# The third of six blocks in the first experts' layer: seven block products for eight

## The chip, the cores and the metric

The kernel runs on one core of one Trainium2 chip. The metric is the time of the program on the device in microseconds (us). Three runs of the kernel before gave 904.05, 906.33 and 907.38 us; the median, 906.33 us, is the time to beat. The profile is that of one execution.

## The reference

Attention over 4 batches, 8 heads, 512 local and 32 global positions, head width 64, gives x with 4 x 544 = 2176 rows of 512 numbers. Two gated layers with 1536 inner columns follow, and only the first layer is touched here:

```
def _moe_ref(x, w_gate, w_val, w_out, rms_g):
    rms = np.sqrt(np.mean(x * x, axis=-1, keepdims=True) + 1e-06)
    xn = x / rms * rms_g
    g = xn @ w_gate
    silu = g * (1.0 / (1.0 + np.exp(-g)))
    val = xn @ w_val
    return silu * val @ w_out

def _moe2_ref(x, w_gate, w_val, w_out):
    gate = 1.0 / (1.0 + np.exp(-(x @ w_gate)))
    return gate * (x @ w_val) @ w_out
```

## The kernel before, in words

**Tiling.** The 1536 inner columns of a layer are cut into six blocks of 256, so the program has blocks g = 0 to 11, and blocks 0 to 5 are the first layer's. The 2176 tokens lie in three parts q = 0, 1, 2 of 768, 768 and 640 columns (`xhi`, `xlo`: 16-bit upper and lower half of x; in listings `xhi_73`, `xhi_74`, `xhi_75` with `xlo_76`, `xlo_77`, `xlo_78` are the parts 0, 1, 2). Every product is three products of 16-bit halves: upper by upper, upper by lower, lower by upper. The sums over blocks are kept in `yacc` (`ya_79`, `ya_80`, `ya_81` for parts 0, 1, 2).

**A plain block** (g < `GS`): for each of six chunks of tokens (five of 384, the last of 256) `gv_mm` makes four results (two column halves `j`, gate and value) of 12 matmuls each, `gv_post` turns them into `hhi` and `hlo`, and `outs` multiplies them with w_out: four results of 6 matmuls, each evicted into `yacc` by VectorE (DVE). Banks of PSUM come from the pool `ps`, eight of one bank each (`b` in the rows). A chunk's `outs` come one chunk later; those of the last two chunks come behind the loop, in `flush`.

**A seven-product block** (g >= `GS`, but for block 6): `quad_gv` works on one part q, cut into two token halves and two column halves, and makes four result blocks for gate and four for value from seven products each (`prod`, 6 passes of two 128-row halves = 12 matmuls over both; 84 matmuls in all, of 384 columns for parts 0 and 1 and of 320 for part 2). Its banks are four pairs (`pp`, `p` in the rows). It needs two things that a plain block doesn't: four sums and differences of the weight blocks (`sums`, into `sm` and `wf`, then `wc`), and four of the tokens' blocks, `tt`.

**The token sums** are made once for the layer, by `x_combos` and `combos`: for each part q two units (`kt` = 0, 1). A unit is, in this order: an addition on GpSimd (POOL) beside one on DVE into the buffer `xb`, two subtractions on DVE, one on POOL, two upper halves on ScalarE (ACT), two lower halves on POOL (`tt<-xb`). There is one buffer `xb`, so a unit begins when the one before is through. The six units wait as entries in `jobs`.

**What sets the order.** The attention stage has its own list of tasks; it takes in chunks of blocks 0 and 1 as they become ready. What is left of the plain blocks then runs in a loop. Between matmuls the loop calls `tick`, which hands out weight conversion (`c_ops`, `s_ops`) and `jobs` by due time (`plan_starts`, `due_w`, `due_j`) to the other engines, if a cost model says that there is room (`fits`). The engines' queues are strictly in that order. Behind the loop stand the lines that matter here:

```
        for q in range(3):
            j_need(q, 1)
        flush()
        st_p0.close()
```

`j_need` writes down whatever is left of the six units, `flush` the last two chunks' `outs`, and only then the seven-product blocks begin, with their own PSUM pairs. The profile's rows carry one line number, L128, since one helper records all operations; so tiles' names are what tells them apart.

Of the kernel before, what the change touches and what calls it, by code (L numbers as in the profile page):

```python
# [21 lines left out]
def tile_attention_moe_moe(  # L22
# [17 lines left out]
    now = dict.fromkeys(("e", "d", "a", "p", "s", "port", "dma"), 0.0)  # L40
# [144 lines left out]
    pb = {}  # L185
# [34 lines left out]
    w_src = [(w1_gate, w1_val, w1_out), (w2_gate, w2_val, w2_out)]  # L220
    wide = w1_gate.dtype == mybir.dt.int64

    GS = 3

    GP = 6
    raw_t = []
# [54 lines left out]
    def w_shift(n, j):  # L281
        u = w_f[n].bitcast(I32)
        v = u if j is None else u[:, j]
        nc.vector.tensor_scalar(out=v, in0=v, scalar1=3, scalar2=None, op0=ALU.logical_shift_left)

    def w_sign(n, j):
        u = w_f[n].bitcast(I32)[:, j]
        nc.vector.scalar_tensor_tensor(out=u, in0=w_words[n][j][:, :, 1], scalar=-0x80000000, in1=u,
                                       op0=ALU.bitwise_and, op1=ALU.bitwise_or)

    def w_low(n, j):
        u = w_f[n].bitcast(I32)[:, j]
        nc.vector.scalar_tensor_tensor(out=u, in0=w_words[n][j][:, :, 0], scalar=29, in1=u,
                                       op0=ALU.logical_shift_right, op1=ALU.bitwise_or)
        w_used[0] += 1
        if j == 1:
            w_words.pop(n)
            conv_done.add(n)

    def w_hi(f, hi):  # L300
        nc.scalar.activation(out=hi, in_=f, func=AF.Copy, scale=WS)

    def w_lo(f, hi, lo):
        nc.vector.scalar_tensor_tensor(out=lo, in0=f, scalar=WS, in1=hi, op0=ALU.mult, op1=ALU.subtract)
# [9 lines left out]
    conv_done, gv_over = set(), set()  # L314
    w_done = {}

    def conv(n):
# [13 lines left out]
        def scale(j):  # L331
            return Op("a", lambda: w_scale(n, j), g, w, ins=raw_in, ok=lambda: len(raw_t) > 0, free=True)

        def bits(j):
            r = [Op("d", lambda: w_sign(n, j), g, w), Op("d", lambda: w_low(n, j), g, w, label=(n, j))]
            return ([Op("d", lambda: w_shift(n, j), g, w)] if g < GS else []) + r

        c_ops.append(Op(None, start, g, w, ok=lambda: len(f_live) < 2, label=None if wide else (n, 1)))
        if wide and g < GS:
            c_ops.extend([scale(0), *bits(0), scale(1), *bits(1)])  # L340
# [3 lines left out]
    def split(n):  # L344
        g, w = divmod(n, 3)
        n_wo = 2 if g < GS else 3

        def ready_in():
            return n in conv_done

        def room():
            if not ready_in():
                return False
            if w == 2:
                return len([x for x in wo_live if (x < GS) == (g < GS)]) < n_wo
            return w == 1 or g < 2 or (bool(pb) or g < GS) and (g < 5 and g != 2 or (0 if g == 2 else g - 2) in gv_over)

        def alloc():
            if w == 2:
                wo_live.append(g)  # L360
                w_t[g][1] = (hp if g < GS else pb[1]).tile([128, 2, 2, DM], F16, tag="wo", name="wo", bufs=n_wo)
            elif w == 0 and g < GS:
                w_t[g] = [hp.tile([128, 2, 2, 2, DM], F16, tag="wgv", name="wgv"), None]
            elif w == 0:
                w_t[g] = [pb[1].tile([128, 2, 2, 7, 256], F16, tag="wc", name="wc", bufs=2), None]

        def over():
            w_f.pop(n)
            f_live.remove(n)

        def mark():
            if w > 0:
                w_done[g][w - 1] = True

        s_ops.append(Op(None, alloc, g, w, ok=room))
        if w == 2 or g < GS or g == GP:
            def dst(a):
                if w == 2:
                    return w_t[g][1][:, :, a]
                if g < GS:  # L380
                    return w_t[g][0][:, :, w, a]
                return w_t[g][0][:, w, a, 0:4].rearrange("p (j a) f -> p j (a f)", j=2)

            def lo():
                w_lo(w_f[n], dst(0), dst(1))
                over()
                mark()
            s_ops.extend([Op("a", lambda: w_hi(w_f[n], dst(0)), g, w, label=(n, 0)), Op("d", lo, g, w, label=(n, 1))])
        else:
            box = []  # L390

            def sums(i):
                if i == 0:
                    box.extend([w_f[n].rearrange("p j (a f) -> p (j a) f", a=2),
                                pb[1].tile([128, 3, 256], F32, tag="sm", name="sm")])
                x, sm = box
                o, i0, i1, op = ((sm[:, 0], x[:, 0], x[:, 2], ALU.subtract), (x[:, 2], x[:, 2], x[:, 3], ALU.add),
                                 (sm[:, 1], x[:, 2], x[:, 0], ALU.subtract), (sm[:, 2], x[:, 1], sm[:, 1], ALU.subtract))[i]
                ES[i].tensor_tensor(out=o, in0=i0, in1=i1, op=op)

            def hi(i):
                w_hi(box[i], w_t[g][0][:, w, 0, (0, 4)[i]:(4, 7)[i]])

            def lo(i):
                a, b = (0, 4)[i], (4, 7)[i]
                w_lo(box[i], w_t[g][0][:, w, 0, a:b], w_t[g][0][:, w, 1, a:b])
                if i == 0:
                    over()
                else:
                    mark()  # L410

            s_ops.extend([Op(e, lambda i=i: sums(i), g, w) for i, e in enumerate(ESN)])
            s_ops.extend([Op("a", lambda: hi(0), g, w), Op("d", lambda: lo(0), g, w), Op("a", lambda: hi(1), g, w),
                          Op("d", lambda: lo(1), g, w, label=(n, 1))])
# [16 lines left out]
    starts = {}  # L431
# [6 lines left out]
    def due_j(key):  # L438
        q, k = key
        left = sum(len(x[1]) for x in jobs if x[0] == key)  # L440
        if k == 0:
            t = starts[GP, q]
        else:
            t = min(t for (g, p), t in starts.items() if p == q and g not in (2, GP) and t > now["e"])
        return t - STEP * left

    def w_need(g, i):
# [1043 lines left out]
    def give():  # L1491
        while True:
            w_give()
            c = []
            for key, ops in (("c", c_ops), ("s", s_ops)):
                if ops:
                    c.append((due_w(ops), key, ops, 0))
            for k in range(2):
                i = [i for i, x in enumerate(jobs) if x[0][1] == k]
                if i:  # L1500
                    key = jobs[i[0]][0]
                    if k == 0 or not any(x[0] == (key[0], 0) for x in jobs):
                        c.append((due_j(key), key, jobs, i[0]))
            for _, key, js, i in sorted(c, key=lambda x: x[0]):
                op = js[i][1][0] if js is jobs else js[0]
                if fits(key, op):
                    if js is jobs:
                        js[i][1].pop(0)
                        if not js[i][1]:
                            js.pop(i)  # L1510
                    else:
                        js.pop(0)
                    run_op(key, op)
                    break
            else:
                return
# [97 lines left out]
```

## Time and profile before

| | |
|---|---|
| median of three runs | 906.33 us (904.05 to 907.38) |
| span of the profiled execution | 903.2 us |
| TensorE (PE) busy | 878.9 us, 97% |
| DVE, ACT, POOL busy | 632.2, 367.4, 288.1 us |
| mean granted TensorE clock | 0.998 |

The span runs from the first instruction to the last; a time of its own for the profiled execution is not listed apart from it, and the three runs lie 0.9 to 4.2 us above it. Busy is the sum of the time in which an engine has at least one instruction running; the idle time of an engine that nobody waits for costs nothing.

### The profile page before, as it was taken

The numbers are of one execution on the slowest core, as the hardware profiler recorded it, in microseconds if no ns is written. First come the engines' busy times: TensorE is split into PE (matmuls) and PEld (weight loads), VectorE is DVE, ScalarE is ACT, GpSimd is POOL, SyncE is SP. The second block draws the span as 40 slices with busy tenths as digits, with TensorE's granted clock in tenths as the row PEclk, the third lists the DMA queues.
The fourth block names the chain that finished last, engine by engine and source line by source line (L and its number), as shares of the span: only waits on it lengthen the run. The fifth ranks groups of instructions, "written<-read, shape, count | busy, mean of one in ns | idle before, by whom it ended". The sixth has DMA issues, their size and how long they took to land.

```text
span 903.2 us, 18734 instructions
## 1 busy us (share of the span) xinstructions
PE 878.9 (97%) x7875; PEld 556.7 (62%) x7875; DVE 632.2 (70%) x922; ACT 367.4 (41%) x697; POOL 288.1 (32%) x320
## 2 busy tenths in 40 slices
PE   8898889999999999999999999999999999999998
PEld 7676666666666666666666666556556565556553
DVE  5977687874765558769959788758778487785352
ACT  4686566756233333222325353443532143322120
POOL 6435454333524641212134424332211313212020
PEclk9999999999999999999999999999999999999999
DMA  9979888331201202100200130020321002000102
GB/s 207 218 164 174 162 184 217 92 97 48 73 21 47 70 24 92 50 1 24 91 27 1 47 94 24 27 91 24 117 88 53 1 1 94 24 1 1 70 24 105
DMA packets 94180, 67.15 MB, mean 74 GB/s; under 512 B 59280, under 2 KB 84368, under 8 KB 94096
## 3 DMA queue, kind: packets, MB, share of 16 engines
q1 hardware_dynamic: 94096, 65.95, 28.7%
q8 instruction: 62, 1.02, 0.5%
q14 instruction: 22, 0.18, 0.1%
HBM read 52.17 MB, written 4.46 MB: 63 GB/s over the span
## 4 chain that ended last, share of the span: by engine, by line
PE 90%; DVE 3%; ACT 2%; DMA 2%; issue 1%; POOL 1%; SPq 1%; ACTq 0%; POOLq 0%; DVEq 0%
PE p L128 61%; PE b L128 28%; DVE x L128 1%; POOL ms L128 1%; ACT pt L128 1%; DMA k<-in_k_l_dram 1%; SPq L128 1%; ACT s L128 1%; DMA q<-in_q_l_dram 1%; DVE mx L128 0%; DMA vt<-in_v_l_dram 0%; DVE wf L128 0%; DVE vw L128 0%; DVE ya L128 0%; ACT ya L128 0%
## 5 line engine op out<-in xcount | busy, mean ns | idle before, releaser
L128 PEld LDWEIGHTS <-wc 128*128 128x128 f16 x2304 | 225.3, 98 | 130.1 <-issue 0.3
L128 PE MATMUL p<-xhi,wc 128*128 128x384 f16 (+1 forms) x768 | 200.9, 317 | 0.2 <-DVE ya L128 0.2
L128 PE MATMUL p<-tt,wc 128*128 128x384 f16 (+1 forms) x1152 | 200.5, 317 | 0.0
L128 POOL TENSOR_TENSOR h<-V,h 128x768 f16<-128x768 f32 (+1 forms) x48 | 75.9, 1602 | 274.5 <-ACT h L128 274.5
L128 PE MATMUL b<-xhi,wgv 128*128 128x384 f16 (+1 forms) x576 | 139.2, 318 | 0.0
L128 PE MATMUL p<-wo,h 128*128 128x512 f16 x612 | 133.4, 379 | 0.0
L128 PE MATMUL p<-xlo,wc 128*128 128x384 f16 (+1 forms) x384 | 121.8, 317 | 0.0
L128 DVE SCALAR_TENSOR_TENSOR wf<-raw,wf 128x512 int32<-128x512 int32 x144 | 112.3, 788 | 2.1
L128 PEld LDWEIGHTS <-wo 128*128 128x128 f16 x864 | 84.4, 98 | 47.5
L128 PEld LDWEIGHTS <-wgv 128*128 128x128 f16 x864 | 83.9, 98 | 46.3 <-issue 0.2
L128 PEld LDWEIGHTS <-h 128*128 128x128 f16 x612 | 59.8, 98 | 71.1 <-POOL h L128 0.3
L128 PE MATMUL b<-xlo,wgv 128*128 128x384 f16 (+1 forms) x288 | 91.4, 317 | 0.0
L128 DVE SCALAR_TENSOR_TENSOR ya<-p,ya 128x768 f32<-128x768 f32 (+3 forms) x42 | 42.6, 1018 | 68.9 <-PE p L128 68.8
L128 ACT ACTIVATE h<-V 128x1536 f16<-128x1536 f32 (+3 forms) x30 | 36.9, 1231 | 103.7 <-DVE V L128 103.7
L128 ACT ACTIVATE sa<-p 128x384 f32<-128x384 f32 (+1 forms) x48 | 22.6, 471 | 125.6 <-PE p L128 109.2
L128 PE MATMUL b<-hhi,wo 128*128 128x384 f16 (+1 forms) x288 | 70.0, 317 | 0.0
L128 PE MATMUL p<-h,wo 128*128 128x384 f16 (+1 forms) x432 | 67.3, 317 | 0.0
L128 DVE TENSOR_TENSOR V<-p,V 128x768 f32<-128x768 f32 (+3 forms) x72 | 56.6, 786 | 11.8 <-PE p L128 9.7
L128 ACT ACTIVATE wf<-raw 128x512 f32<-128x512 f32 x72 | 48.0, 676 | 40.4 <-DVE wc L128 18.1
L128 POOL COPY vw<-vt 32x520 f32<-32x520 f32 (+1 forms) x61 | 47.2, 775 | 53.4 <-PE b L128 34.5
L128 POOL TENSOR_TENSOR hlo<-t,hhi 128x384 f16<-128x384 f32 (+1 forms) x36 | 34.9, 970 | 86.9 <-ACT hhi L128 86.9
L128 DVE TENSOR_TENSOR G<-p,G 128x768 f32<-128x768 f32 (+3 forms) x72 | 56.5, 784 | 7.4 <-PE p L128 5.4
(122 smaller groups left out, 1117.4 us busy)
## 6 DMA issues: line engine op xcount, KB each, us to landing
raw<-in_moe_w_gate_dram SPq DMA_DIRECT2D x24, 512.0 KB, 3.9
raw<-in_moe_w_val_dram SPq DMA_DIRECT2D x24, 512.0 KB, 3.6
raw<-in_moe_w_out_dram SPq DMA_DIRECT2D x24, 512.0 KB, 3.8
vw<-vt SPq DMA_DIRECT2D x28, 260.0 KB, 5.8
k<-in_k_l_dram SPq DMA_DIRECT2D x16, 256.0 KB, 5.0
q<-in_q_l_dram SPq DMA_DIRECT2D x16, 256.0 KB, 6.0
vt<-in_v_l_dram SPq DMA_DIRECT2D x32, 128.0 KB, 5.2
out_dram<-ya SPq DMA_DIRECT2D x16, 256.0 KB, 2.3
```

What stands on the lines that cost most here:

```text
L128: return f(*args, **kw)
```

## The change

`GS` goes from 3 to 2: block 2 leaves the plain blocks and becomes a seven-product block. Two conditions that had the 3 written out in numbers now follow `GS`.

```
-    GS = 3
+    GS = 2
...
-            return w == 1 or g < 2 or (bool(pb) or g < GS) and (g < 5 and g != 2 or (0 if g == 2 else g - 2) in gv_over)
+            return w == 1 or g < GS or bool(pb) and (g < GS + 2 or g - 2 in gv_over)
...
-            t = min(t for (g, p), t in starts.items() if p == q and g not in (2, GP) and t > now["e"])
+            t = min(t for (g, p), t in starts.items() if p == q and g >= GS and g != GP and t > now["e"])
```

The loop over plain blocks now ends with block 1, and the planner places everything anew. Two places show it, on DVE and POOL, where the plain blocks end and the first product of seven follows.

DVE before, from the last gated results `t` of the last plain block (block 2) to its last evictions into `ya_81` (`wf`, `sm`, `wc` are weight conversion):

```order
L128 SCALAR_TENSOR_TENSOR t<-b,t 128x256
L128 SCALAR_TENSOR_TENSOR ya_81<-b,ya_81 128x384
L128 SCALAR_TENSOR_TENSOR wf<-raw,wf 128x512
L128 SCALAR_TENSOR_TENSOR ya_81<-b,ya_81 128x384 x2
L128 TENSOR_TENSOR sm<-wf 128x256
L128 SCALAR_TENSOR_TENSOR ya_81<-b,ya_81 128x384
L128 TENSOR_TENSOR sm<-wf,sm 128x256
L128 SCALAR_TENSOR_TENSOR ya_81<-b,ya_81 128x256
L128 SCALAR_TENSOR_TENSOR wc<-wf,wc 128x1024
L128 SCALAR_TENSOR_TENSOR ya_81<-b,ya_81 128x256 x3
```

DVE now, from the same place (the last plain block is block 1) to the first sum of a seven-product block, `G<-p,sa`:

```order
L128 SCALAR_TENSOR_TENSOR t<-b,t 128x256
L128 TENSOR_TENSOR xb<-xhi_75,xlo_78 128x2x320
L128 TENSOR_TENSOR xb<-xb 128x2x320
L128 TENSOR_TENSOR xb<-xb 128x320
L128 TENSOR_TENSOR xb<-xhi_75,xlo_78 128x2x320
L128 TENSOR_TENSOR xb<-xb 128x2x320
L128 TENSOR_TENSOR xb<-xb 128x320
L128 SCALAR_TENSOR_TENSOR ya_81<-b,ya_81 128x384 x4
L128 SCALAR_TENSOR_TENSOR ya_81<-b,ya_81 128x256 x4
L128 TENSOR_TENSOR G<-p,sa 128x768
```

The DVE halves of part 2's two token units now stand between the last `t` and the eight evictions; before, they stood a chunk and more ahead of that place, among the evictions of earlier chunks.

POOL before, from part 2's second unit to the first lower half of a seven-product block:

```order
L128 TENSOR_TENSOR xb<-xhi_75,xlo_78 128x2x320
L128 TENSOR_TENSOR wf<-wf 128x256
L128 TENSOR_TENSOR hlo<-t,hhi 128x384 x2
L128 TENSOR_TENSOR xb<-xb 128x320
L128 TENSOR_TENSOR tt_4921<-xb,tt_4921 128x2x320 x2
L128 TENSOR_TENSOR hlo<-t,hhi 128x384
L128 TENSOR_TENSOR hlo<-t,hhi 128x256
L128 TENSOR_TENSOR sm<-wf 128x256
L128 TENSOR_TENSOR hlo<-t,hhi 128x256
L128 TENSOR_TENSOR wf<-wf 128x256
L128 TENSOR_TENSOR h_5412<-V,h_5411 128x768 x2
```

POOL now, from the lower halves `hlo` of the last plain chunk on (`tt_4328` is `tt` of part 1, `tt_4668` that of part 2):

```order
L128 TENSOR_TENSOR hlo<-t,hhi 128x256 x2
L128 TENSOR_TENSOR tt_4328<-xb,tt_4328 128x2x384 x2
L128 TENSOR_TENSOR xb<-xhi_75,xlo_78 128x2x320
L128 TENSOR_TENSOR xb<-xb 128x320
L128 TENSOR_TENSOR tt_4668<-xb,tt_4668 128x2x320 x2
L128 TENSOR_TENSOR xb<-xhi_75,xlo_78 128x2x320
L128 TENSOR_TENSOR xb<-xb 128x320
L128 TENSOR_TENSOR tt_4668<-xb,tt_4668 128x2x320 x2
L128 TENSOR_TENSOR h_4765<-V,h_4764 128x768 x2
```

The end of part 1's second unit and both units of part 2 now stand behind the last `hlo` of the plain blocks. On SyncE's queue one load of a weight half moves behind four small copies; nothing else changes there.

## Rows read from the trace of the kernel before

**Rows 1.** The page: span, and busy time of each engine.

```profile
span 903.2 us, 18734 instructions
PE 878.9 (97%) x7875; PEld 556.7 (62%) x7875; DVE 632.2 (70%) x922; ACT 367.4 (41%) x697; POOL 288.1 (32%) x320
```

**Rows 2.** The chain that ended last: start us, us, what.

```profile
345.80 0.34 DVE ya L128
...
346.18 552.70 PE p L128 x3348
```

**Rows 3.** Stretches: length; PE, PEld, DVE, ACT, POOL busy; clock; DMA.

```profile
193.00:343.40 150.40, 150.31 (x990) 96.88 (x991) 91.22 (x144) 57.40 (x105) 69.54 (x60) 1.00 0.15 46
346.20:500.00 153.80, 153.80 (x996) 97.41 (x996) 122.18 (x143) 51.45 (x61) 36.32 (x25) 1.00 0.13 42
```

**Rows 4.** Timeline of PE at the end of block 1: start us, us, instructions.

```profile
263.84 0.33 PE L128 MATMUL b<-hhi,wo 128*128 128x384 f16 x1
...
267.74 0.27 PE L128 MATMUL b<-xhi,wgv 128*128 128x256 f16 x1
...
272.98 0.33 PE L128 MATMUL b<-hhi,wo 128*128 128x384 f16 x1
```

**Rows 5.** Timeline of ACT in the first seven-product block: first products of part 2.

```profile
382.36 0.44 ACT L128 ACTIVATE sa<-p 128x320 f32<-128x320 f32 x1 [4.29 <-PE p L128]
388.00 0.44 ACT L128 ACTIVATE sa<-p 128x320 f32<-128x320 f32 x1 [5.21 <-PE p L128]
```

**Rows 6.** PE, then POOL, at the end of block 2.

```profile
339.34 0.33 PE L128 MATMUL b<-hhi,wo 128*128 128x384 f16 x1
...
340.60 0.67 POOL L128 TENSOR_TENSOR hlo<-t,hhi 128x256 f16<-128x256 f32 x1 [1.27 <-ACT hhi L128]
```

**Rows 7.** Timeline of POOL: operations of the token units.

```profile
207.60 3.25 POOL L128 TENSOR_TENSOR tt<-xb,tt 128x768 f16<-128x768 f32 x2
...
229.93 3.69 POOL L128 TENSOR_TENSOR tt<-xb,tt 128x768 f16<-128x768 f32 x2
...
298.37 1.74 POOL L128 TENSOR_TENSOR xb<-xhi,xlo 128x640 f32<-128x640 f16 x1
...
309.01 0.86 POOL L128 TENSOR_TENSOR xb<-xb 128x320 f32<-128x320 f32 x1 [3.05 <-DVE xb L128]
...
316.96 1.40 POOL L128 TENSOR_TENSOR xb<-xhi,xlo 128x640 f32<-128x640 f16 x1
...
329.48 2.38 POOL L128 TENSOR_TENSOR tt<-xb,tt 128x640 f16<-128x640 f32 x1
332.01 1.40 POOL L128 TENSOR_TENSOR tt<-xb,tt 128x640 f16<-128x640 f32 x1 [0.15 <-ACT tt L128]
```

**Rows 8.** Timeline of DVE: token units, evictions, a weight conversion twice.

```profile
230.39 1.73 DVE L128 SCALAR_TENSOR_TENSOR wf<-raw,wf 128x512 int32<-128x512 int32 x1
...
235.49 0.67 DVE L128 SCALAR_TENSOR_TENSOR wf<-raw,wf 128x512 int32<-128x512 int32 x1
...
286.75 0.74 DVE L128 SCALAR_TENSOR_TENSOR ya<-b,ya 128x256 f32<-128x256 f32 x2
...
298.76 1.47 DVE L128 SCALAR_TENSOR_TENSOR ya<-b,ya 128x384 f32<-128x384 f32 x3
...
322.10 0.81 DVE L128 TENSOR_TENSOR xb<-xb 128x640 f32<-128x640 f32 x1
...
323.77 0.48 DVE L128 TENSOR_TENSOR xb<-xb 128x320 f32<-128x320 f32 x1
```

**Rows 9.** Timeline of PE: the end of its longest wait.

```profile
78.39 0.63 PE L128 MATMUL b<-ident,k 128*128 128x128 f32 x4 [2.08 <-DMA k<-in_k_l_dram]
```

**Rows 10.** Stretches of half a microsecond behind it, columns as in rows 3.

```profile
79.50:80.00 0.50, 0.50 (x4) 0.10 (x1) 0.45 (x1) 0.38 (x2) 0.50 (x1) 0.68 1.10 202
80.00:80.50 0.50, 0.50 (x5) 0.20 (x5) 0.00 (x0) 0.00 (x0) 0.44 (x2) 0.50 1.01 208
...
83.00:83.50 0.50, 0.50 (x49) 0.49 (x30) 0.41 (x1) 0.00 (x0) 0.00 (x0) 0.90 1.39 176
```

## The prediction

> **What bounds the kernel now.** I read the page first: PE is busy for 878.9 of 903.2 us, DVE for 632.2, ACT and POOL for less than 370 [rows 1]. Then the chain that ended last: behind the attention stage PE's matmuls are the chain, and from 346.18 us it is one piece of 552.70 us in which PE waits for nobody; this is all the seven-product work [rows 2]. The stretch before it, with block 2 as a plain block, is as full: PE 150.31 of 150.40 us [rows 3]. So a column less on PE is time won, as long as nothing new makes PE wait; and any new wait is paid whole, since there is no idle time of PE to take it up. The one joint between plain and seven-product work shows how a wait would arise: the chain goes from DVE's eviction `ya` (345.80, 0.34 us) to PE's first product of seven at 346.18 [rows 2]. That product waits for a bank that DVE has to empty, and before the change DVE was there in time. The reader should see in these rows a PE that is full on both sides of a joint, and a joint that hangs on DVE.
>
> **The change on PE.** Pitches come from gapless pieces: 24 matmuls of 384 columns from 263.84 to 267.74, so 162.5 ns each; 48 of 256 from 267.74 to 272.98, so 109.2 ns [rows 4]; 42 of 320 from 382.36 to 388.00, so 134.3 ns [rows 5].
> Removed: block 2's plain gate and value, 240 matmuls of 384 (39.0 us) and 48 of 256 (5.24 us), together 44.2 us.
> Added: 168 of 384 (27.3 us) and 84 of 320 (11.3 us), together 38.6 us.
> The output products go from 120 of 384 and 24 of 256 (22.1 us) to 96 of 384 and 48 of 320 (22.0 us).
> Sum on PE: 5.7 us less.
>
> **Its work on the other engines.** The weight sums of block 2 (four small ones, and two splits for one, per matrix), the twelve wide additions on DVE per part, and the later conversion of block 3's weights lie beside matmuls. DVE is busy 61% of the plain stretch and 79% of the seven-product one (91.22 of 150.40, 122.18 of 153.80), POOL 46 and 24% [rows 3]. I cost them at nothing; the price if that cover fails is a rival below. The moved load on SyncE goes past four small copies and feeds block 3's weights, wanted some 60 us later.
>
> **The joint.** The six token units are spread through the plain stretch: the first `tt` starts at 207.60 us, the last at 332.01 [rows 7]. Now the plain loop ends a block earlier, and two and a half units are left over. The orders show them between the last gated result and the eight evictions on DVE, and behind the last `hlo` on POOL. The eight output results of the last two chunks fill all eight banks, so the first product of seven can't start before DVE empties banks, and DVE reaches the first eviction only when POOL and DVE are nearly through both units of part 2. I walk through it from T0, the moment when PE ends block 1's last gate and value results: 272.98 us in this trace [rows 4]. PE's order up to there hardly changes, so I keep the number.
> - PE's own work behind T0: 24 matmuls of 384 and 24 of 256, 3.9 + 2.6 = 6.5 us, so PE is free at T0 + 6.5.
> - POOL ends the last `hlo` at T0 + 1.9: at the end of block 2 the same step took from 339.34 to 340.60 + 0.67 [rows 6].
> - Two `tt` of part 1: 3.25 us (3.69 with DVE in the way) [rows 7]. T0 + 5.2.
> - The two additions of part 2's first unit: POOL 1.40, DVE 0.82. Both wait for the last `tt`, so both want to start at once. Side by side they take POOL's 1.40 to 1.74 [rows 7]; one behind the other 2.2. For the choice there is the conversion `wf`, 0.67 us alone but 1.73 us when it starts 0.46 us into POOL's `tt` pair [rows 7, 8]: an instruction of DVE with two inputs in SBUF waits for POOL's running one. I take 2.2. T0 + 7.4.
> - DVE's two subtractions, 0.81 + 0.48 [rows 8], 0.1 for the hops; POOL's 0.86; two `tt` at 1.40 (1.40 to 2.38 [rows 7]). T0 + 12.4.
> - The second unit as far as DVE's last subtraction: 2.2 + 1.4. T0 + 16.0.
> - Eight evictions: three of 384 take 1.47, so 0.46 each; two of 256 take 0.74, so 0.33 each [rows 8]; four and four, with their tail, 3.25 us, and 0.05 to PE. T0 + 19.3.
> PE so stands for 19.3 - 6.5 = 12.8 us. DVE's and ACT's queues can't go round it: what is behind the evictions on DVE is the seven-product work itself and block 3's weights.
> Ends for this term: additions side by side twice (-1.3) and a wait for the sixth eviction rather than the eighth (-0.66) give 10.8. The slow `tt` and additions all over (0.45 + 2 x 0.35 + 1.43) give 15.4.
>
> [...]
>
> **The clock.** PE's longest wait in this trace is 2.08 us, up to 78.39 [rows 9]. [...] I take 1.7, and 3.4 as the upper end, if the low clock lasts twice as long.
>
> **Sum.** -5.7 + 12.8 + 1.7 = +8.8 us on a span of 903.2, so 912.0. The median of the runs lies 3.1 us above the span; with the same distance 906.3 + 8.8 = 915.1 us. Ends: -5.7 + 10.8 + 1.7 = +6.8 and -5.7 + 15.4 + 3.4 = +13.1, so 913.1 to 919.4.
>
> **Rivals.**
> 1. *The wait is covered, and only PE's saving is left*: 906.3 - 5.7 = 900.6, faster. It needs POOL's and DVE's 2.5 units done by T0 + 6.5. For it: POOL is idle half of the plain stretch [rows 3]. Against it: POOL's queue is strictly in order and holds these units behind an `hlo` that can't exist before T0 + 1.9; the shortest durations of all rows still make 15.5 us from there to the last eviction. It decides where wait and clock together fall under 5.7 us.
> 2. *The wait is there, but half as long*, if the eight evictions or the first pair's banks don't hang on the last unit: a first product that could start behind one unit, at T0 + 19.3 - 6.4, gives a wait of 6.4 and with the clock 906.3 + 2.4 = 908.7, no change that could be told.
> 3. *DVE becomes the bound in block 2*. DVE enters the seven-product stage behind: before, block 3's weights were all converted at the joint, now half of them. Block 2 brings DVE about 36 us (per part four additions each for gate and value, one gating product and four evictions), and what is left of block 3's conversion about 15, in 60 us of PE; 85%, against 79% now. Where DVE's order bunches, PE's four pairs (6.8 us of products) could run full. A bunch of conversions of 3 to 4 us makes 918 to 919.
> 4. *The low clock lasts*: 916.8 with 3.4 us.
> 5. *The attention stage shifts*. Its end is reordered a little, as block 2's weights are converted in other pieces there. PE is already nearly full by then; I give it 1 us either way.
>
> **Chances.** The forecast with its bounds and the lasting clock 0.74, DVE as bound 0.13, half the wait 0.09, covered 0.04. A measurement of this kernel can tell about 0.5%, 4.5 us, from no change: faster ends at 901.8, slower begins at 910.9. From the cases: slower 0.87, same 0.09, faster 0.04. The range takes the bounds, 913.1 to 919.4, widened by the runs' own spread (904.05 to 907.38 round 906.33): 911 to 920. Inside it lies the forecast with most of rival 3.
>
> **What would show it.** In the changed profile: the seven-product products of block 2 at the same pitches, 252 matmuls of gate and value; the plain stretch full up to about 279.5 us; then a gap of PE of 11 to 15 us, ended by DVE's last `ya`, with POOL's `tt` and DVE's `xb` in a chain inside it; a granted clock of 0.50 for some 3.4 us behind it; then a full piece of PE of about 615 us to the end. Wrong would be: no gap, or one under 8 us (units run earlier than the queues allow, or banks free without the evictions), additions that run side by side, a clock that stays up, or more gaps inside block 2.

## The result and the profile after

The changed kernel takes 916.08 us (median of four runs, 913.78 to 919.08), the kernel before 905.19 us in the same comparison (four runs, 902.93 to 907.38). The ratio is 1.0123, with a 95% interval of 1.0093 to 1.0153: slower by 1.2%. The forecast was 915.1 us with a range of 911 to 920. That is +8.8 us on 906.33 us, the median of the first three of these four runs of before; the measured difference is 10.9 us.

The page of the changed kernel, its span and engines (answers to rows 1):

```profile
span 914.9 us, 18657 instructions
PE 875.8 (96%) x7839; PEld 553.4 (60%) x7839; DVE 657.0 (72%) x929; ACT 369.5 (40%) x686; POOL 291.2 (32%) x318
```

PE has 36 matmuls fewer and is busy for less time, and still the span is 11.7 us longer. So PE must stand somewhere. Its waits behind 180 us, by what ended them (us in total, times, longest):

```profile
PE p L128 <- DVE ya L128: 12.3, 1, 12.3
PE b L128 <- DVE x L128: 1.8, 2, 1.1
PE b L128 <- DVE ya L128: 1.4, 1, 1.4
```

One wait of 12.3 us, where the kernel before waits 0.2 us at the same step, from DVE's `ya` to PE's first product of seven [rows 2]. The other two lines lie ahead of 197 us and come back below. The chain that ended last shows what lies in it (start us, us, what):

```profile
276.59 0.43 DVE t L128
...
277.05 0.43 ACT hhi L128
...
277.54 0.67 POOL hlo L128
278.21 3.21 POOL tt L128 x2
...
281.49 2.04 POOL xb L128
...
283.55 0.84 DVE xb L128
...
284.41 0.50 DVE xb L128
...
284.98 0.86 POOL xb L128
285.84 2.72 POOL tt L128 x2
...
288.62 2.04 POOL xb L128
...
290.69 0.84 DVE xb L128
...
291.55 0.49 DVE xb L128
292.04 3.19 DVE ya L128 x8
```

This is the predicted walk, step by step: the last `hlo`, the half unit of part 1, both units of part 2, the eight evictions. The reader sees that no engine is busy all the time; what makes it long is that POOL, DVE and POOL again take turns on one buffer. PE's last plain product ends at about 283.0, its first product of seven starts at 295.27.

The granted clock around it (stretches of half a microsecond, columns as in rows 3; answers to rows 10):

```profile
284.50:285.00 0.50, 0.00 (x0) 0.00 (x0) 0.40 (x1) 0.50 (x1) 0.02 (x1) 1.00 0.00 0
285.00:285.50 0.50, 0.00 (x0) 0.00 (x0) 0.00 (x0) 0.14 (x1) 0.50 (x1) 0.69 0.00 0
...
295.00:295.50 0.50, 0.23 (x1) 0.10 (x1) 0.22 (x1) 0.00 (x0) 0.50 (x1) 0.50 0.00 0
298.00:298.50 0.50, 0.50 (x3) 0.22 (x2) 0.00 (x0) 0.00 (x0) 0.00 (x0) 0.50 0.00 0
298.50:299.00 0.50, 0.50 (x4) 0.26 (x3) 0.00 (x0) 0.00 (x0) 0.00 (x0) 0.66 0.00 0
```

It falls 2.2 us into the wait and stays at 0.50 for the first 3.6 us of PE's work behind it, from 295.27 to about 298.84 (the 0.66 of the last row, split into 0.50 and 1.00). The first twelve products, from 295.27 to 298.96, take 3.69 us, where twelve at the predicted 162.5 ns take 1.95: 1.7 us lost.

What the forecast did not have is the time T0 at which PE ends block 1's gate and value results. It was 272.98 us before [rows 4] and is 276.32 here. From T0 to the end of the span the kernel before takes 903.2 - 272.98 = 630.2 us, the changed one 914.9 - 276.32 = 638.6: 8.4 us more, where -5.7 + 12.8 + 1.7 = 8.8 were forecast. The other 3.3 us lie ahead of T0. In the timeline of DVE the end of the attention stage looks like this in the changed kernel:

```profile
192.24 0.69 DVE L128 TENSOR_SCALAR wf<-wf 128x1024 int32<-128x1024 int32 x1 [1.70 <-ACT wf L128]
192.97 2.75 DVE L128 SCALAR_TENSOR_TENSOR wf<-raw,wf 128x512 int32<-128x512 int32 x4
195.63 0.74 DVE L128 SCALAR_TENSOR_TENSOR ya<-ya,ms,gB 128x512 f32<-128x512 f32 x1
```

and like this in the kernel before:

```profile
190.41 1.42 DVE L128 SCALAR_TENSOR_TENSOR wf<-raw,wf 128x512 int32<-128x512 int32 x2
192.28 0.75 DVE L128 SCALAR_TENSOR_TENSOR ya<-ya,ms,gB 128x512 f32<-128x512 f32 x1 [0.46 <-POOL ms L128]
```

The last scaling of the global tokens, `ya<-ya,ms,gB`, is what PE's plain work needs next. Before, DVE waited 0.46 us for its input `ms`; now a whole weight's shift and four bit steps stand ahead of it in the queue, and it starts 3.35 us later. PE's timeline of the same stage shows that this is one wait of three. Before:

```profile
177.96 0.71 PE L128 MATMUL b<-ident,ya 128*128 128x128 f32 x5
178.50 0.83 PE L128 MATMUL b<-ident,s 128*128 128x128 f32 x4
179.53 0.77 PE L128 MATMUL b<-vw,pt 128*32 128x65 f32 x32 [0.20 <-ACT pt L128]
180.24 0.66 PE L128 MATMUL b<-ident,x 128*128 128x128 f32 x4
...
193.09 0.66 PE L128 MATMUL b<-ident,ya 128*128 128x128 f32 x4 [0.37 <-DVE ya L128]
```

Now:

```profile
178.55 0.71 PE L128 MATMUL b<-ident,ya 128*128 128x128 f32 x5
180.39 0.66 PE L128 MATMUL b<-ident,x 128*128 128x128 f32 x4 [1.13 <-DVE x L128]
...
188.55 0.63 PE L128 MATMUL b<-ident,x 128*128 128x128 f32 x4 [0.71 <-DVE x L128]
...
196.43 0.65 PE L128 MATMUL b<-ident,ya 128*128 128x128 f32 x4 [1.40 <-DVE ya L128]
```

PE's own order has changed too: `ident,s` and the first `vw,pt`, which stood ahead of `ident,x`, now stand behind it. From the mark in the first row, the five `ident,ya`, to T0 it was 95.02 us (177.96 to 272.98) and is 97.77 (178.55 to 276.32): 2.75 us more. The remaining 0.6 us lie ahead of the mark. The orders that were compared ahead of the prediction leave this stage out. Whether the 2.75 us are the change or the spread between executions, two traces can't tell; the experiments do.

### The profile page after: what moved, and what is told of

It is laid out like the page before. It is cut to its first block, busy times and chain, and to the rows that moved or that the text cites. A ratio compares the mean times of both kernels' runs of the same rounds, so it can differ in the third digit from the quotient of the medians.

```text
span 914.9 us, 18657 instructions
## 1 busy us (share of the span) xinstructions
PE 875.8 (96%) x7839; PEld 553.4 (60%) x7839; DVE 657.0 (72%) x929; ACT 369.5 (40%) x686; POOL 291.2 (32%) x318
## 4 chain that ended last, share of the span: by engine, by line
PE 84%; DVE 5%; DMA 4%; POOL 2%; ACT 2%; issue 1%; SPq 1%; POOLq 0%; ACTq 0%; DVEq 0%
PE p L128 67%; PE b L128 17%; DMA vt<-in_v_l_dram 2%; DVE x L128 1%; DVE wf L128 1%; POOL ms L128 1%; ACT pt L128 1%; DMA raw<-in_moe_w_val_dram 1%; SPq L128 1%; DMA q<-in_q_l_dram 1%; POOL tt L128 1%; POOL xb L128 1%; DVE ya L128 1%; DMA raw<-in_moe_w_out_dram 0%; DVE den L128 0%
## 5 line engine op out<-in xcount | busy, mean ns | idle before, releaser
L128 PEld LDWEIGHTS <-wc 128*128 128x128 f16 x2556 | 250.5, 98 | 157.5 <-issue 14.4
L128 PE MATMUL p<-xhi,wc 128*128 128x384 f16 (+1 forms) x840 | 221.0, 318 | 12.3 <-DVE ya L128 12.3
L128 PE MATMUL p<-tt,wc 128*128 128x384 f16 (+1 forms) x1296 | 226.4, 318 | 0.0
L128 POOL TENSOR_TENSOR h<-V,h 128x768 f16<-128x768 f32 (+1 forms) x54 | 88.0, 1651 | 303.7 <-ACT h L128 303.7
L128 PE MATMUL b<-xhi,wgv 128*128 128x384 f16 (+1 forms) x384 | 94.3, 319 | 0.3 <-issue 0.3
L128 PE MATMUL p<-h,wo 128*128 128x384 f16 (+1 forms) x576 | 89.9, 317 | 0.0
L128 PEld LDWEIGHTS <-wgv 128*128 128x128 f16 x576 | 55.9, 98 | 31.1 <-issue 1.3
L128 PE MATMUL b<-xlo,wgv 128*128 128x384 f16 (+1 forms) x192 | 61.1, 318 | 0.0
L128 PE MATMUL b<-hhi,wo 128*128 128x384 f16 (+1 forms) x192 | 46.9, 317 | 0.0
L128 DVE SCALAR_TENSOR_TENSOR V<-V,G 128x1536 f32<-128x1536 f32 (+1 forms) x27 | 45.4, 1682 | 1.9
```

The lines of the kernel that those rows point to most:

```text
L128: return f(*args, **kw)
```

## Experiments

The theory: the loss is the wait at the joint (token units left over there), the clock behind it, and a later end of the attention stage from the order in which block 2's weights are converted. Rivals: the wait belongs to block 2's own products; the clock falls for another reason; the attention stage's shift is only spread; DVE is the bound in block 2.

**1. Units held back, block 2 plain.** An edit of the kernel before, in `give`:

```
-                i = [i for i, x in enumerate(jobs) if x[0][1] == k]
+                i = [i for i, x in enumerate(jobs) if x[0][1] == k and x[0] != (2, 1)]
```

> The kernel before (block 2 stays plain) with one edit: the two token units of part 2 are not handed out ahead of time, so that they stand behind the last lower half of the plain blocks on POOL and between the last gated result and the eight evictions on DVE, as in the changed kernel. Theory (the wait at the joint comes from units left over there, whatever the block is): two units are left for the two and a half of the changed kernel; its walk of 18.95 us from the last gated product to the first product of seven loses the half unit's pair of lower halves, 3.28 us, so 15.7 us, of which 6.6 are covered by the last chunk's plain products: PE waits about 9 us, the granted clock reads 0.50 for some 3.4 us behind it (1.7 us lost), and the kernel is 10 to 11 us slower than before, about 915.5 us. Rival (the wait belongs to the seven-product block 2: its weights or its products' sums come late): no wait of PE over 1 us at the joint and a time within 2 us of before.

Measured: 927.7 us, 1.0255 times before (1.0231 to 1.0279), twice the loss that the theory gave. PE's waits behind 180 us tell why:

```profile
PE p L128 <- DVE ya L128: 7.7, 1, 7.7
PE p L128 <- ACT tt L128: 5.9, 2, 4.3
PE p L128 <- POOL tt L128: 4.9, 2, 3.4
```

The wait at the joint is there, 7.7 us. The two others lie in the second layer: its units of part 2 have the same name in `jobs`, so the edit held them back too. Only the first line speaks to the question; so the run was made again with the edit limited to the first layer.

**2. The same, in the first layer alone.**

```
+                i = [... and (x[0] != (2, 1) or starts[GS, 0] < now["e"])]
```

> The run with part 2's units held back again, with the holding back limited to the first layer: in the first try it also held back the second layer's units, which made two more waits of PE there. Theory (units left over at the joint make the wait, whatever block 2 is): one wait of PE of 7.7 us at the joint, as in the first try, with 1.7 us of clock behind it, no other new wait, and 904.2 + 9.4 = 913.6 us, 1.0104 times before. Rival (something else in the first try's order cost the time): a time that differs from this by more than 3 us.

Measured: 914.54 us, 1.0100 (1.0071 to 1.0129), one wait of 7.7 us, `PE p <- DVE ya`, and nothing else new. From T0 to the end 914.6 - 275.25 = 639.4 us, 9.2 more than before, for 9.4 forecast. The loss can be had without the change itself: units left over at the joint are enough.

**3. PE kept at work in the wait.** The changed kernel, with the last plain result computed 18 times over:

```
+            last_one = gr == [1] and key == chunks_b[-1] and d == 3
-            for g in gr:
+            for g in gr * (18 if last_one else 1):
+                c = 0 if last_one or g == gr[0] else c
```

> The changed kernel, with the last plain result before the joint computed 18 times over into the same bank (the last of them counts, so the output is the same): PE works some 10.9 us longer where it waited 12.3, and nothing else waits for it, since DVE evicts that bank last. Theory (the clock is lost because PE stands idle): the granted clock stays at 1.00 behind the joint, or falls for under 1 us, the first product of seven starts at the same distance from the last gated product (18.95 us), and the kernel is 1.7 us faster than the changed kernel (914.4 for 916.1, 1.0102 times before for 1.0123). Rival (the clock falls by something else, such as the load of the first products of seven): the same stretch of 3.4 us at 0.50, and no gain.

Measured: 914.22 us, 1.0102 (1.0078 to 1.0127); the clock reads 1.00 in every half microsecond from 280 to 295. The restart in PE's timeline, at full speed after a rest of 1.15 us:

```profile
290.61 0.32 PE L128 MATMUL p<-xhi,wc 128*128 128x384 f16 x1 [1.15 <-DVE ya L128]
```

T0 is 271.65 here, so the walk takes 18.96 us for 18.95, and T0 to the end 636.9 us: 1.7 less than in the changed kernel. The ratio alone could not have told 1.7 us; the distance from T0 does.

**4. Evictions ahead of the units.** The changed kernel with two steps exchanged:

```
+        flush()
         for q in range(3):
             j_need(q, 1)
-        flush()
```

> The changed kernel with the two steps at the joint exchanged: the last chunks' plain products and evictions are written ahead of the left-over units. Theory (two things hang on the units: DVE's eight evictions by queue order, and the first seven-product sums, whose buffers lie in xb's space): the first four pairs of seven-product results (6.8 us of PE) start within 1.5 us of the last plain product, then PE waits some 5 to 6 us until POOL's last lower half of part 2 is done, some 20 us from the last gated product; 5 to 6 us come back, 910 to 911 us, 1.005 to 1.007 times before. Rival (only the evictions are in the way): no second wait, 12 to 14 us come back, 902 to 904 us. Other rival (the first products themselves wait for the units): PE waits as long as in the changed kernel, 916 us.

Measured: 910.53 us, 1.0072 (1.0048 to 1.0096). PE's timeline:

```profile
285.29 0.32 PE L128 MATMUL p<-xhi,wc 128*128 128x384 f16 x1 [0.80 <-DVE ya L128]
...
298.78 0.48 PE L128 MATMUL p<-xhi,wc 128*128 128x384 f16 x1 [6.50 <-ACT sa L128]
```

The first pairs start at once, seven products run, and then PE waits 6.5 us for the first `sa`, which can only be written when POOL's last `tt` has left `xb`. So the units hold up the joint twice, by DVE's queue and by the buffer's space. That the second wait is a wait for space follows from the order of the two in the chain (`tt` ends at 298.2, `sa` starts at 298.24; ACT itself was through with its part of the units at 296.28); it was not tried with another place for `sa`. T0 to the end is 634.5 us, 4.1 less than in the changed kernel: waits of 0.8 and 6.5 us and 2.5 us of lost clock stand where 12.3 and 1.7 stood.

**5. The attention stage alone.** The kernel before with block 2's weights converted in the changed kernel's pieces, in `conv`:

```
-            return ([Op("d", lambda: w_shift(n, j), g, w)] if g < GS else []) + r
+            return ([Op("d", lambda: w_shift(n, j), g, w)] if g < 2 else []) + r
...
-        if wide and g < GS:
+        if wide and g < 2:
```

> The kernel before (block 2 stays plain) with block 2's weights converted in the pieces of the changed kernel: both scalings of a weight first, then one shift over both halves, for two of each in turn; this also reorders the attention stage as the changed kernel does. Theory (the later end of the attention stage in the changed kernel is made by this order: the load of a weight half and its conversions on DVE come ahead of the global tokens' last scaling): the last gated product of block 1 comes 3 us later than before (at about 276 us for 272.98), and the kernel is some 3 us slower, 1.003 times before. Rival (that shift is the spread between executions): 272.5 to 273.5 us and the time of before, 1.000.

Measured: 907.34 us, 1.0033 (1.0016 to 1.0050), 3.2 us slower between the medians and 3.0 by the ratio. T0 is 276.31, and DVE's rows are those of the changed kernel:

```profile
192.95 2.75 DVE L128 SCALAR_TENSOR_TENSOR wf<-raw,wf 128x512 int32<-128x512 int32 x4
195.62 0.74 DVE L128 SCALAR_TENSOR_TENSOR ya<-ya,ms,gB 128x512 f32<-128x512 f32 x1
```

**6. The reverse.** The changed kernel with the same two conditions set to `g < 3`, so that the pieces are those of before.

> The changed kernel with block 2's weights converted in the pieces of the kernel before (scale, shift, two of bits, half by half), which sets the attention stage's order back to that of before. Theory (that order costs 3.2 us): the last gated product of block 1 within 1.5 us of 273 us, the wait at the joint 12 to 13 us as in the changed kernel, and 916.1 - 3.2 = 912.9 us, 1.009 times before. Rival (the shift is only the spread between executions): 916 us, 1.012.

Measured: 912.82 us, 1.0094 (1.0072 to 1.0116), T0 272.94, the wait 12.3 us, T0 to the end 638.2. Beside the changed kernel's 1.0123 the intervals overlap, so the time by itself doesn't settle it. The way from the mark to T0 does: it is back at 95.03 us.

**7. Units early.** The changed kernel, in `due_j` and `fits`:

```
+            if starts[GS, 0] > now["e"]:
+                t = starts[GS, 0]
+                left = sum(len(x[1]) for x in jobs if x[0][1] == 1)
...
-        sl = SLACK
+        sl = SLACK if isinstance(op, Op) or starts[GS, 0] < now["e"] else 3000
```

> The changed kernel with the planner's rule for the token units altered: all of them are due when block 2's first product starts, and each may be handed out up to 3000 ns ahead of its engine by the planner's cost model, for 1000. In the queues all six units then stand ahead of the last plain chunk's lower halves on POOL and ahead of the last evictions on DVE. Theory (the wait and the clock are all that the joint costs): no wait of PE over 1 us at the joint, granted clock 1.00 there, and 916.1 - 12.3 - 1.7 + 0.7 = 902.8 us, 0.9985 times before; what the attention stage lost stays. Rival (the room isn't there: what the units had left to do turns up as waits among the plain evictions, or as late weights for blocks 2 and 3): waits of PE between 190 and 350 us that add up to 4 us or more, 907 us or slower.

Measured: 903.94 us, 1.0002 (0.9981 to 1.0022), T0 275.53, T0 to the end 627.9 us. The wait of 12.3 us is gone and the clock stays up (1.000 on the mean), but small waits have come in: 2.6 us (0.70, 0.32, 0.46 and 1.08) between 290 and 302, for `G`, `V` and `sa`. So the theory holds for the joint and misses these waits. The edit alters the due time and the room to hand out ahead together; which of the two was needed was not tried.

**8. Units early, pieces of before.** Both edits, 6 and 7.

> The same with block 2's weights converted in the pieces of the kernel before, so that both costs are taken away and the seven products are left: 902.8 - 3.2 = 899.6 us, 0.995 times before, with the last gated product of block 1 within 1.5 us of 273 us and PE full from there to the end. Rival (as for the run before): 904 us or slower.

Measured: 901.69 us, 0.9968 (0.9950 to 0.9987), T0 272.28, T0 to the end 628.1 us. The full PE that was expected isn't there: it still waits three times in the first 20 us of block 2, in its timeline:

```profile
287.65 1.14 PE L128 MATMUL p<-tt,wc 128*128 128x384 f16 x6 [0.89 <-DVE G L128]
295.61 1.14 PE L128 MATMUL p<-tt,wc 128*128 128x384 f16 x6 [0.97 <-DVE V L128]
298.80 2.12 PE L128 MATMUL p<-tt,wc 128*128 128x384 f16 x12 [1.08 <-DVE V L128]
```

And DVE is nearly full there, by stretches:

```profile
190.00:272.00 82.00, 81.62 (x543) 52.88 (x541) 35.01 (x58) 30.21 (x57) 52.03 (x43) 1.00 0.05 14
...
285.00:290.00 5.00, 4.11 (x26) 2.39 (x25) 4.61 (x7) 2.67 (x4) 0.00 (x0) 1.00 0.67 194
290.00:300.00 10.00, 7.95 (x49) 4.49 (x48) 9.02 (x14) 4.06 (x5) 1.45 (x2) 1.00 0.37 113
```

The units took the weights' turn in the planner, and the conversions piled up behind the joint, though DVE was busy only 43% of the plain stretch.

**9. Room for the conversions.** One number more: up to the joint, weight conversion may also be handed out 2000 ns ahead.

```
-        sl = SLACK if isinstance(op, Op) or starts[GS, 0] < now["e"] else 3000
+        sl = SLACK if starts[GS, 0] < now["e"] else 2000 if isinstance(op, Op) else 3000
```

> The run before (units early, block 2's weights in the pieces of before) with one number altered: up to the joint the planner may hand out weight conversion 2000 ns ahead of its engine, for 1000. On DVE the order then has three conversion steps and a shift (some 3.3 us) between the last eviction of the plain blocks and the first sum of a seven-product block, for twelve steps (some 8 us) in the run before. Theory (the 3.0 us that PE waits in the first 20 us of block 2 there come from conversions of weights that the units pushed to the joint on DVE, rival 3 of the prediction in small): under 1 us of such waits is left, and 901.7 - 2.5 = 899.2 us, 0.994 times before. Rival (DVE is short of time there in any order): 2 us or more of waits on G or V, or on evictions ahead of the joint, and 901 to 903 us.

Measured: 899.26 us, 0.9954 (0.9927 to 0.9981), the fastest of all. PE's waits behind 180 us:

```profile
PE b L128 <- DVE ya L128: 0.4, 1, 0.4
PE p L128 <- DVE ya L128: 0.2, 1, 0.2
```

T0 to the end is 892.9 - 268.00 = 624.9 us, 5.3 less than before: nearly all of the 5.7 that the seven products were to save.

The distance from T0 to the end in every kernel, worked out from T0 (the first product with w_out behind block 1's last gate and value results, in PE's timeline) and the span:

| kernel | T0 | span | T0 to end | against before |
|---|---|---|---|---|
| before | 272.98 | 903.2 | 630.2 | |
| changed | 276.32 | 914.9 | 638.6 | +8.4 |
| 2 units held, plain block 2 | 275.25 | 914.6 | 639.4 | +9.2 |
| 3 PE kept at work | 271.65 | 908.5 | 636.9 | +6.7 |
| 4 evictions first | 277.81 | 912.3 | 634.5 | +4.3 |
| 5 other pieces, plain block 2 | 276.31 | 907.3 | 631.0 | +0.8 |
| 6 pieces of before | 272.94 | 911.1 | 638.2 | +8.0 |
| 7 units early | 275.53 | 903.4 | 627.9 | -2.3 |
| 8 both | 272.28 | 900.4 | 628.1 | -2.1 |
| 9 both, with room | 268.00 | 892.9 | 624.9 | -5.3 |

The last column hardly moves where only the attention stage differs (0.8 between before and run 5, 0.4 between changed and run 6), so it tells the joint's terms apart to under a microsecond. T0 itself moves by several microseconds between executions (268.00 to 275.25 with the pieces of before, 271.65 to 277.81 with the changed kernel's), so that the attention term can't be read from the T0 of one pair of traces. From the mark, the five `ident,ya`, to T0 it can: 95.02 or 95.03 us in all six traces with the pieces of before (the kernel before and runs 1, 2, 6, 8 and 9), and 97.77 or 97.78 in all five with the larger pieces (the changed kernel and runs 3, 4, 5 and 7). So the pieces and the order that comes with them cost 2.75 us, and in each of the five PE has the same three waits of 1.13, 0.71 and 1.40 us. The spread of T0 lies ahead of the mark, which comes at 172.98 to 180.22 us; what makes it was not looked into. The medians of three pairs that differ in the pieces agree, each within its noise: 3.0 us (run 5 against before, interval 0.16 to 0.50%), 0.29% or 2.6 us (changed against run 6), and 2.3 us (run 7 against run 8).

## Why the prediction was right, and where it was not

- **PE's saving, -5.7**: right. Where no wait is left (run 9) T0 to the end is 5.3 us shorter. Of the sum's terms it is the only one that belongs to the seven products.
- **The joint, 12.8 (10.8 to 15.4)**: right, 12.3, with the predicted steps in the predicted order. The walk took 18.95 us for 19.3. Of the two additions of each unit I had said that one follows the other, 2.2 us. They do, in 2.1, but it is POOL's that is late: DVE starts at 281.44 and takes 0.82, POOL starts at 281.49 and takes 2.03, where 1.40 was its time alone [rows 7]. In both units DVE starts first, by 0.05 and 0.04 us, and POOL ends some 1.25 us behind DVE's end. In the row of `wf` at 230.39 [rows 8] DVE was the one that started second: its 1.73 us end at 232.12, 0.55 us behind the end of POOL's first `tt` (229.93 and 1.64 us).
- **That it is left-over units**: shown by runs 2 (units alone make it) and 7 (without them it is gone). Not block 2's weights or products.
- **The clock, 1.7 (to 3.4)**: right in cause; run 3 takes the idle time away and gets 1.7 back. No run shows 1.7 us as what any wait costs: in the trace of before the clock read 0.50 for 3.4 us behind the wait of 2.08 us [rows 9, 10], which is 1.7 us of work, but behind waits of 12.3 us it read 0.50 for 3.6 us (changed kernel, 1.7 lost) and for 2.8 (run 6, 1.4 lost), and run 4 lost 2.5 behind one of 6.5. That the size was met so exactly is in part luck.
- **Rival 2, half the wait**: it saw one of the two things that hold the joint up. Run 4 shows that first products can start without the units once the evictions are in front; what then stops PE is, by the order of the rows, the space of `xb`.
- **Rival 3, DVE as bound in block 2**: not in the changed kernel, which has no further wait of PE there; DVE is busy 45.83 of 53.00 us from 300 to 353, 86% for the 85% forecast. But it is near: where the units go first, the weights' conversions come late, and 2.6 to 3.0 us of such waits appear (runs 7 and 8), from conversions in a bunch, as the rival put it. DVE had time for both in the plain stretch: with more room to hand out both ahead, run 9 has none of these waits left. So it was the planner's rules that kept one of the two back, the units in the changed kernel, the weights in runs 7 and 8.
- **Rival 5 and "PE's order up to there hardly changes, so I keep the number"**: this is the term that was mis-sized, 1 us either way for a measured 2.75. The reason given is wrong in two places. PE's order does change, at 178 to 182 us: it now comes to `ident,x` before `x` is there and waits 1.13 us, though DVE scales that `x` no later behind the mark than before (1.04 us, for 1.31). And the load that moves (182.04 us before, 186.55 now) is not one of block 3's: counted along SyncE's queue, it is the second half of block 2's value weights, whose conversion is what was reordered. The third wait (1.40 for 0.37) comes from DVE's queue, where the larger piece puts a shift and four bit steps in front of the scaling that PE waits for. Why the second `x` is late (0.71 us, at 188.55) was not taken apart. Followed on both queues, as the prediction did at the joint, the order would have shown the first and the third.

From the mark to the end the changed kernel takes 914.9 - 178.55 = 736.35 us and the kernel before 903.2 - 177.96 = 725.24: 11.1 us more, and -5.7 + 12.3 + 1.7 + 2.75 = 11.05. So four terms, three of them forecast, account for the whole; with the 5.3 us that run 9 measured for the 5.7 that were worked out they miss it by 0.4. That 915.1 came within 1 us of 916.08 is luck in part: the forecast difference was +8.8 for a measured 10.9, and the missed 2.1 us are half hidden because the kernel before ran at 905.19 us in the comparison, 1.1 less than the median that the 8.8 was added to.

## What to carry to other kernels

Where a stage is replaced by a cheaper one, ask which preparation had been hidden behind the old one: here 44 us of plain products were also the time in which the token units got done, and taking them away turned a saving of 5 us into a loss of 8, until the planner's rules for the units were altered. Follow the queues at every place that the change reorders, not only at the one where it is aimed; a conversion costed at nothing stood in front of an instruction that PE waited for. And where the start of a kernel makes its span vary by microseconds from run to run, measure the rest from a mark behind it, and one stage between two marks: 2.75 us showed in every trace that way, and in the times only near the noise.

## What the runs showed of the hardware

The granted clock did not fall at one fixed time after PE stopped. Read from stretches of half a microsecond (a reading between 0.50 and 1.00 split into the two), over one wait each, it fell 2.2 us into the idle time in the changed kernel (283.0 to 285.2), 4.8 in run 6 (279.6 to 284.4), 4.0 in run 2 (348.3 to 352.3) and 4.7 in run 4 (292.3 to 297.0); after the restart it stayed at 0.50 for 3.6, 2.8, 3.2 and 5.1 us. So a wait of 6.5 us lost more clock (2.5 us of work) than two of 12.3 (1.7 and 1.4), and rests of 0.80 us (run 4) and 1.15 us (run 3) lost none, with a clock of 1.00 in every half microsecond from 283 to 288 and from 288 to 293.
